# Attention beside a dense layer: odd heads' scores in a step of their own, and a new order of the loads

## The chip, the cores and the metric

One NeuronCore of a Trainium2 chip runs the whole program. Its engines work side by side, each through its own instructions in order: TensorE (PE, matmuls into PSUM; PEld is its weight load), VectorE (DVE), ScalarE (ACT), GpSimd (POOL) and SyncE (SP), which here only issues DMAs and waits for what they need. The metric is the time of one execution on the device in microseconds, the median of several runs.

## The reference, cut to what matters

Three layers follow each other. The first is a gated linear attention (mLSTM): for each of 4 batches and 8 heads a state C of 40 x 40 is carried over 768 positions.

```
for t in range(S):
    m_new = max(f_gate[t] + m, i_gate[t])
    f_stab, i_stab = exp(f_gate[t] + m - m_new), exp(i_gate[t] - m_new)
    C = f_stab * C + i_stab * outer(v[t], k[t]);  n = f_stab * n + i_stab * k[t]
    y[t] = sigmoid(o_gate[t]) * (C @ q[t]) / max(abs(n @ q[t]), 1)
```

Then a dense layer over all 3072 positions of width 320, `relu(x @ w_in)**2 @ w_out` with 2048 hidden columns, and at last a layer of 8 experts in which each position goes to the one with the largest logit: `gate * relu(x @ w1[e]) @ w2[e]`.

## The kernel before, in words

**Chunks.** The attention is done by chunks of 128 positions, 6 for each of the 4 batches, 24 in all, numbered 0 to 23 in the order in which they are worked on. Within a chunk the recurrence becomes matmuls: scores of all pairs of positions (k against q, for each head), times a decay matrix that is the exponential of a masked sum of gates, times the values; to that comes what the state C carries in from the chunk before.

**Names.** st are a chunk's rows of k and q as loaded (two tiles, 120 x 1024 each, in two buffers, so room for one chunk), q3 another copy of q, kvo the rows of k, v and of the gate o (two buffers), Ab the two tiles of decay rows (even and odd heads; four buffers, so room for two chunks). kq holds k and q split into a rounded part and what is left, for exact scores in TensorE's faster format. It has one buffer: line 637 (ScalarE) writes the rounded part of k or q, and four instructions of line 640 (GpSimd) the rest.

**Steps.** `Main.STEPS` cuts a chunk's work into nine steps, of which the last three run beside the first three of the next chunk. Before: step 0 `inter` (the state's part, on TensorE) and all 8 `scores` (line 774: even heads into one PSUM tile sp, odd heads into another), step 1 `weigh0` (VectorE, line 779: even scores times decays) and `scaled`, step 2 `weigh1`, `gate` and `update`, step 3 `update_masked` and `values0`, step 4 `carried` and `values1` (line 787), step 5 `divided`, then `gated` (lines 832 and 833), `turned` (line 835, transposes xpt on TensorE, lines 720 and 722) and `out`. `half` runs one step of the last three of the chunk before (`rest`), then one step of the chunk, and then `prepare`.

**Preparation.** `prepare(n, h)` says what is asked for behind step h of chunk n. `causal` adds and masks decay rows on GpSimd (lines 668 and 669), `decay` takes their exponential on ScalarE (line 675), `decays` loads Ab (line 647), `kvo` (line 616) and `qk` (lines 627 and 630: st and q3) load rows, `round` makes kq. In a chunk of the loop `round(n + 1, 0)` stands behind step 1, `round(n + 1, 1)` behind step 2.

**The dense layer beside it.** It runs in groups of 3 chunks, 16 blocks f to a group. `l1` (line 859) makes 8 matmuls into hp; ScalarE makes g and gh of it (lines 867, 868), VectorE gl (lines 876, 879); `l2` (lines 892 to 894) makes 9 matmuls of gh and gl into the accumulators. Two blocks of `l1` are issued ahead of `l2` (AHEAD = 2). `fin` closes a group: logits lp (line 957), ranks (line 1024), stores of x_d (line 1052).

**Order.** The order on every engine is that in which the code writes the instructions. The chunks 0 to 6 and the first dense blocks follow a list written by hand (PLAN, where the word `sc` calls a chunk's scores); from chunk 7 on `attend` spreads the steps evenly between the dense blocks (STEP = 0.7 of a step at each call, two calls a block). SP's DMAs have that order too, and an issue that has to wait for its buffer holds up the ones behind it.

**PSUM.** Three of eight banks hold the accumulators; all other tiles (hp, sp, tp, pv, xpt, lpt, lp, pr) share the five buffers of psa. A new tile waits until the last reader of the tile that had its buffer is done.

Of the kernel before, what the change touches and what calls it, by code (L numbers as in the profile page):

```python
# [9 lines left out]
F32 = mybir.dt.float32  # L10
# [14 lines left out]
B, H, S, D = 4, 8, 768, 40  # L25
L = 128
# [350 lines left out]
def kernel(ctx, tc, qk, q3, kvo, gates, w_io, wg, w12, cst, out, dbg=None):  # L377
# [8 lines left out]
    def pool(name, bufs, to, **kw):  # L386
        p = tc.tile_pool(name=name, bufs=bufs, **kw)
        to.append(p)
        return p.__enter__()
# [5 lines left out]
    psa = pool("psa", 5, early_ps, space=PSUM)  # L395
# [288 lines left out]

    def prepare(n, h):

        todo = {1: [], 2: [(n + 1, "causal", 0)], 3: [(n + 2, "decays"), (n + 1, "causal", 1), (n + 1, "decay", 0)],
                4: [(n + 1, "decay", 1)], 5: [(n + 1, "weighted")]}
        if n > 0:
            todo[KVO].append((n + 1, "kvo"))  # L690
        if n < WHOLE:
            todo[QK0].append((n + 1, "qk"))
        if n + 1 >= WHOLE:
            for j in range(2):
                todo[(ROUND0 if n < WHOLE else ROUND1)[j]].append((n + 1, "round", j))
            todo[QK1].append((n + 2, "qk"))
        for m, name, *a in todo.get(h, []):
            if m < NC:
                ahead(m, name, *a)
# [3 lines left out]
    def ahead(m, name, *a):  # L703
        if (m, name, *a) not in over:
            over.add((m, name, *a))
            assert name != "decay" or m < AT_ONCE or (m, "causal", *a) in over
            getattr(chunks[m], "decays_early" if name == "decays" and m < AT_ONCE else name)(*a)
# [27 lines left out]
    class Main:  # L735


        STEPS = (("inter", "scores"), ("weigh0", "scaled"), ("weigh1", "gate", "update"), ("update_masked", "values0"),
                 ("carried", "values1"), ("divided",), ("gated",), ("turned",), ("out",))

        def __init__(self, n):
# [10 lines left out]
        def step(self, k):  # L752
            for part in self.STEPS[k]:
                self.run(part)

        def finished(self, k):
            return all(part in self.done or (self.c == 0 and part in ("inter", "scaled", "carried")) for part in self.STEPS[k])

# [4 lines left out]
            if self.last and self.b + 1 < AT_ONCE:  # L763
                nc.sync.dma_start(out=C.rearrange("p g n -> p (g n)"), in_=C_d[self.b + 1])

        def scores(self):
            n, d = self.n, self.d
            assert n < WHOLE or all((n, "round", j) in over for j in range(2))
            for r in range(2):
                self.sps.append(psa.tile([128, 4, L], F32, tag="a", name="sp"))  # L770
            for h in range(H):
                c = slice(L * h, L * h + L)
                k, q = (d.st[j][:, c] for j in range(2)) if n < WHOLE else (d.kq[:, j, c] for j in range(2))
                nc.tensor.matmul(self.sps[h % 2][:, h // 2], k, q, start=True, stop=True)  # L774
# [343 lines left out]
    mains = [Main(n) for n in range(NC)]  # L1118
# [4 lines left out]
    def turn(x, *a):  # L1123
        if count[x] < len(turns[x]):
            fn, i = turns[x][count[x]]
            count[x] += 1
            fn(i, *a)
# [7 lines left out]
    def rest():  # L1135

        n, k = tails
        if n < NC and steps[0] >= PERIOD * (n + 1):
            mains[n].step(PERIOD + k)
            tails[:] = (n, k + 1) if PERIOD + k + 1 < len(Main.STEPS) else (n + 1, 0)  # L1140

    def catch_up():

        while steps[0] < PERIOD * NC and mains[steps[0] // PERIOD].finished(steps[0] % PERIOD):
            steps[0] += 1
        while steps[0] >= PERIOD * (tails[0] + 1) and mains[tails[0]].finished(PERIOD + tails[1]):
            n, k = tails
            tails[:] = (n, k + 1) if PERIOD + k + 1 < len(Main.STEPS) else (n + 1, 0)
        for i in range(steps[0]):
            prepare(*divmod(i, PERIOD))  # L1150
# [18 lines left out]
    def half(n):  # L1169

        if steps[0] < evac(n):
            n, h = divmod(steps[0], PERIOD)
            rest()
            step()
            prepare(n, h)
# [5 lines left out]
    with tc.manual_schedule():  # L1181
# [30 lines left out]
        def layer1():  # L1212
            q = l1(*its[nl[0]])
            gs[nl[0]] = next(q)
            late.append(q)
            late_of[nl[0]] = [q, 0]
            nl[0] += 1

        def layer2():
            i = nd[0]  # L1220
            g, f = its[i]
            if f == 0:
                accs[g] = accumulators()

            if g == NG - 1 and f >= NF - 3:
                l2(g, accs[g], range(2), f, *gs[i])
            elif g == NG and f >= NF0 - 3:
                l2(g, accs[g], [0], f, *gs[i])
                hook()
            else:  # L1230
                for t in range(3):
                    l2(g, accs[g], [t], f, *gs[i])
                    if g == NG:
                        hook()
                gs.pop(i)
            nd[0] += 1
            if (g, f) == (FETCH, 0):
                x = nc.sync.value_load(e0, min_val=0, max_val=E - 1)
                nc.sync.dma_start(out=raw.rearrange("p (o n) -> p o n", o=1), in_=w12[bass.ds(x, 1)].rearrange("o p n -> p o n"))
            if f == NF - 1:  # L1240
                if g == NG - 1:
                    for j in range(i - 2, i + 1):
                        l2(g, accs[g], [2], its[j][1], *gs.pop(j))
                q = fin(g, accs.pop(g))
                next(q)
                before = list(fins)
                fins.append(q)
                if g == NG - 2:
                    leave(brief)
                    p0 = ctx.enter_context(tc.tile_pool(name="p0", bufs=1, side="right"))  # L1250
                    w0.extend([p0.tile([128, WN], F32R, name="w0h"), p0.tile([128, W1], F32R, name="w01l")])
                    fins.append(first_unit(before, p0))
                if g == NG - 1:
                    leave(dense)
                    fins[:] = [last_tokens(q)]
# [27 lines left out]
        def last_tokens(q):  # L1283
# [82 lines left out]
            for j in range(3):  # L1366
# [3 lines left out]
            rest_of.update(idx=idx, xs=xs, gts=gts)  # L1370

        names = dict(kv="kvo", qk="qk", de="decays", ca="causal0", cb="causal1", ea="decay0", eb="decay1", vw="weighted", ra="round0", rb="round1")
        parts = {"in": "inter", "sc": "scores", "wa": "weigh0", "sd": "scaled", "wb": "weigh1", "th": "gate", "up": "update", "um": "update_masked",
                 "va": "values0", "cc": "carried", "vb": "values1", "di": "divided", "ga": "gated", "tu": "turned", "ou": "out"}
        turn_of = {"A": ("A",), "R": ("R",), "T": ("T",), "TP": ("T", "pool"), "TQ": ("T", "psum"), "S": ("S",), "SA": ("S", "scalar"), "W": ("W",), "H": ("H",), "L": ("L",), "LV": ("L", True)}

        def token(word):
            k = len(word.rstrip("0123456789"))
            name, i = word[:k], int(word[k:] or 0)
            if name in turn_of:  # L1380
                x, *a = turn_of[name]
                assert count[x] == i, (word, count[x])
                turn(x, *a)
            elif name in names:
                what = names[name]
                ahead(i, *((what[:-1], int(what[-1])) if what[-1].isdigit() else (what,)))
            elif name in parts:
                mains[i].run(parts[name])
            elif name == "g":
                next(gt)  # L1390
            elif name == "f":
                for _ in range(i):
                    nc.tensor.matmul(apart, ones, ones.rearrange("p (o n) -> p o n", o=1).to_broadcast([128, 4, 128]), start=True, stop=True)
            elif name == "l":
                assert nl[0] == i
                layer1()
            elif name in ("sa", "sb", "sbP"):
                if name == "sbP":
                    on_pool.add(its[i])
                late_of[i][1] += 1  # L1400
                assert late_of[i][1] == (1 if name == "sa" else 2)
                next(late_of[i][0])
                if name != "sa":
                    late.remove(late_of[i][0])
            elif name == "m":
                assert nd[0] == i
                layer2()
            else:
                {"z": constants, "dt": carry}[name]()
# [3 lines left out]
        for word in PLAN:  # L1413
            token(word)
        late.sort(key=lambda q: [i for i in late_of if late_of[i][0] is q])
        catch_up()
        while nd[0] < len(its):
            i = nd[0]
# [135 lines left out]
```

## Time and profile before

| | |
|---|---|
| median of 3 runs | 770.36 us (764.28, 770.36, 772.28) |
| the profiled execution | 762.73 us, of which the span from the first to the last instruction is 760.8 us |
| TensorE | busy 737.1 us (97%), 5197 matmuls |
| VectorE / ScalarE / GpSimd | busy 488.1 / 415.4 / 360.4 us (64 / 55 / 47%) |
| mean granted TensorE clock | 0.993 of full speed |
| DMA | 108.99 MB, 143 GB/s on average |

Busy shares are means over stages with different limits. The opening and the chunks run to some 430 us, the rest of the dense layer to some 530 us, then come the experts. TensorE's matmuls overlap, so its busy time hides small delays; idle time of an engine before an instruction is shown in brackets with what ended it. A wait ended by several events is put down to the last of them.

### The profile page before, as it was taken

Reading aid. Unit: us, or ns where it says so; the run is one execution under the profiler, and the core shown is the slowest. Engines: PE = TensorE matmul, PEld = TensorE weight load, DVE = VectorE, ACT = ScalarE, POOL = GpSimd, SP = SyncE. Lnnn points to the kernel's source line nnn. Section 1 sums busy time; section 2 is a strip of 40 time slices with the busy share of each in tenths; the row PEclk is TensorE's granted clock in tenths of the full one; section 3 lists DMA queues with packets and bytes.
Section 4 is the critical chain, followed back from the end, with each engine's and each line's share of the span. In section 5 each row is a group of like instructions: output and inputs, shape, how many; then the busy total and the mean of one; then the engine's idle time right before and its main releaser. Section 6 shows DMA issues by size and latency. Waiting matters only on the chain.

```text
span 760.8 us, 14426 instructions
## 1 busy us (share of the span) xinstructions
PE 737.1 (97%) x5197; PEld 722.0 (95%) x5198; DVE 488.1 (64%) x1140; ACT 415.4 (55%) x807; POOL 360.4 (47%) x411
## 2 busy tenths in 40 slices
PE   9999999899999999999999999999899999999995
PEld 6799999899999999899989999999799999999995
DVE  8899875865865765565495554454375665777453
ACT  4688865445455545434545435563374556776453
POOL 7658855566446524543554000530246324666540
PEclk9999999999999999999999999999999999999999
DMA  7788844548544444453441000100198556766720
GB/s 245 246 238 262 254 107 120 150 127 271 160 112 129 119 136 111 116 151 104 131 113 69 2 33 1 33 33 33 39 340 265 168 168 204 239 197 197 240 52 14
DMA packets 55043, 108.99 MB, mean 143 GB/s; under 512 B 6896, under 2 KB 34681, under 8 KB 54834
## 3 DMA queue, kind: packets, MB, share of 16 engines
q1 hardware_dynamic: 50370, 95.88, 42.1%
q0 software_dynamic: 4160, 11.77, 4.9%
q8 instruction: 47, 0.77, 0.4%
q10 hardware_dynamic: 432, 0.29, 0.1%
q14 instruction: 34, 0.28, 0.1%
HBM read 98.69 MB, written 10.86 MB: 144 GB/s over the span
## 4 chain that ended last, share of the span: by engine, by line
PE 53%; DVE 4%; DMA 2%; POOL 2%; issue 2%; ACT 1%; SPq 0%; DVEq 0%; POOLq 0%; ACTq 0%
PE hp L291 13%; PE hp L859 12%; PE acc L892 4%; PE acc L894 4%; PE op L310 4%; PE op L312 4%; PE op L311 4%; PE acc L893 4%; DMA st<-in_qk_dram 2%; PE xp L277 1%; PE pv L787 1%; POOL kq L640 1%; PE lp L957 1%; DVE w01l L162 1%; PE sp L774 0%
## 5 line engine op out<-in xcount | busy, mean ns | idle before, releaser
L640 POOL TENSOR_TENSOR kq<-st,kq 120x256 fp32r<-120x256 f32 x136 | 96.2, 740 | 74.7 <-ACT kq L637 71.3
L892 PE MATMUL acc<-w_h,gh 128*128 128x320 f32 x384 | 124.7, 325 | 0.0
L894 PE MATMUL acc<-w_h,gl 128*128 128x320 f32 x384 | 118.9, 310 | 0.0
L893 PE MATMUL acc<-w_l,gh 128*128 128x320 f32 x384 | 118.4, 308 | 0.0
L859 PE MATMUL hp<-xh,w_h 128*128 128x384 f32 x384 | 113.3, 349 | 4.3 <-DVE xh L733 1.6
L867 ACT ACTIVATE g<-hp 128x384 f32<-128x384 f32 x128 | 62.0, 485 | 97.6 <-PE hp L859 93.5
L876 DVE SCALAR_TENSOR_TENSOR hp<-hp,g 128x384 f32<-128x384 f32 x126 | 70.5, 560 | 65.9 <-ACT g L867 65.6
L260 DVE SCALAR_TENSOR_TENSOR gl<-hp,gh 128x384 fp32r<-128x384 f32 x88 | 47.6, 553 | 68.1 <-ACT gh L230 67.7
L859 PE MATMUL hp<-xh,w_l 128*128 128x384 f32 x384 | 87.8, 336 | 0.0
L859 PE MATMUL hp<-xl,w_h 128*128 128x384 f32 x256 | 87.1, 340 | 0.0
L879 DVE TENSOR_TENSOR gl<-hp,gh 128x384 fp32r<-128x384 f32 x126 | 70.3, 558 | 14.1 <-DVE hp L876 0.5
L893 PEld LDWEIGHTS acc<-w_l,gh 128*128 128x128 f32 x384 | 72.5, 189 | 0.0
L892 PEld LDWEIGHTS acc<-w_h,gh 128*128 128x128 f32 x384 | 72.4, 189 | 0.0
L894 PEld LDWEIGHTS acc<-w_h,gl 128*128 128x128 f32 x384 | 72.2, 188 | 0.0
L859 PEld LDWEIGHTS hp<-xh,w_h 128*128 128x128 f32 x384 | 65.7, 190 | 5.4 <-ACT signs L563 1.8
L868 ACT ACTIVATE gh<-g 128x384 fp32r<-128x384 f32 x128 | 67.2, 525 | 4.6 <-PE acc L893 0.5
L859 PEld LDWEIGHTS hp<-xh,w_l 128*128 128x128 f32 x384 | 69.3, 189 | 0.0
L230 ACT ACTIVATE gh<-hp 128x384 fp32r<-128x384 f32 x88 | 43.2, 491 | 39.1 <-PE hp L291 38.2
L637 ACT ACTIVATE kq<-st,cs 120x1024 fp32r<-120x1024 f32 x34 | 39.0, 1146 | 39.5 <-DMA st<-in_qk_dram 35.8
L675 ACT ACTIVATE Ab<-Ab 128x512 f32<-128x512 f32 x42 | 26.2, 628 | 54.0 <-POOL Ab L669 53.9
L681 POOL TENSOR_TENSOR vw<-kvo,wT 128x378 f32<-128x378 f32 x20 | 17.6, 879 | 77.3 <-DMA kvo<-in_kvo_dram 57.0
L173 POOL DMA_INDIRECT out_dram<-ot,idx x34 | 40.1, 1180 | 27.0 <-ACT ot L209 19.6
(291 smaller groups left out, 1861.4 us busy)
## 6 DMA issues: line engine op xcount, KB each, us to landing
st<-in_qk_dram SPq DMA_DIRECT2D x34, 480.0 KB
raw<-in_w_dram SPq DMA_DIRECT2D x30, 512.0 KB, 4.9
kvo<-in_kvo_dram SPq DMA_DIRECT2D x24, 529.0 KB
raw<-in_w_io_dram SPq DMA_DIRECT2D x16, 704.0 KB
Ab<-A_d SPq DMA_DIRECT2D x42, 256.0 KB
raw<-in_w_dram SPq DMA_DIRECT2D x20, 427.0 KB, 4.4
raw<-in_w_dram SPq DMA_DIRECT2D x10, 426.0 KB, 4.3
q<-in_q_dram SPq DMA_DIRECT2D x20, 180.0 KB
```

Source lines behind the costliest of these rows:

```text
L230: e.activation(out=gh[:, j], in_=hp[j % 4], func=ACTF.Relu).then_inc(sGH, 1)
L260: e.scalar_tensor_tensor(out=gl[:, j], in0=hp[j % 4], scalar=0.0, in1=gh[:, j].bitcast(F32), op0=ALU.max, op1=ALU.subtract).then_inc(sGL, 1)
L291: m = e.matmul(hp[f % 4][:, 0:w], a, c, start=(n == 0), stop=(n == 7))
L640: nc.gpsimd.tensor_tensor(out=o[:, c], in0=self.st[j][:, c], in1=o[:, c].bitcast(F32), op=ALU.subtract)
L859: nc.tensor.matmul(hp, a, x, start=(n == 0), stop=(n == 7))
L867: nc.scalar.activation(out=r, in_=hp, func=ACTF.Relu)
L868: nc.scalar.activation(out=gh, in_=r, func=ACTF.Square)
L876: e.scalar_tensor_tensor(out=sq, in0=hp, scalar=0.0, in1=r, op0=ALU.max, op1=ALU.mult)
L879: e.tensor_tensor(out=gl, in0=sq, in1=gh.bitcast(F32), op=ALU.subtract)
L892: nc.tensor.matmul(acc[t][:, 0:DM], gh[:, sl], wh, start=(f == 0), stop=False)
L893: nc.tensor.matmul(acc[t][:, 0:DM], gh[:, sl], wl, start=False, stop=False)
L894: nc.tensor.matmul(acc[t][:, 0:DM], gl[:, sl], wh, start=False, stop=end)
```

## The change

The odd heads' scores move from step 0 to step 1 of a chunk, behind `weigh0` and `scaled`; each PSUM tile sp is taken when its four heads are due. In `prepare`, the decay rows of chunk n + 2 are asked for behind step 4 instead of step 3, so that in SP's queue `kvo` of n + 1 and `qk` of n + 2 (step 3) come first. PLAN keeps its words: `sc` now calls both halves one after the other, even heads first.

```
     def prepare(n, h):
-        todo = {1: [], 2: [(n + 1, "causal", 0)], 3: [(n + 2, "decays"), (n + 1, "causal", 1), (n + 1, "decay", 0)],
-                4: [(n + 1, "decay", 1)], 5: [(n + 1, "weighted")]}
+        todo = {1: [], 2: [(n + 1, "causal", 0)], 3: [(n + 1, "causal", 1), (n + 1, "decay", 0)],
+                4: [(n + 2, "decays"), (n + 1, "decay", 1)], 5: [(n + 1, "weighted")]}
...
-        STEPS = (("inter", "scores"), ("weigh0", "scaled"), ("weigh1", "gate", "update"), ("update_masked", "values0"),
+        STEPS = (("inter", "scores0"), ("weigh0", "scaled", "scores1"), ("weigh1", "gate", "update"), ("update_masked", "values0"),
...
-        def scores(self):
+        def scores(self, r):
             n, d = self.n, self.d
             assert n < WHOLE or all((n, "round", j) in over for j in range(2))
-            for r in range(2):
-                self.sps.append(psa.tile([128, 4, L], F32, tag="a", name="sp"))
-            for h in range(H):
+            self.sps.append(psa.tile([128, 4, L], F32, tag="a", name="sp"))
+            for h in range(r, H, 2):
...
+            elif name == "sc":
+                mains[i].run("scores0")
+                mains[i].run("scores1")
```

## Rows read from the trace of the kernel before

**Rows 1.** Busy us (and instructions) by engine, clock, DMA share, GB/s, 105 to 430 us

```profile
105.00:430.00 325.00, 316.69 (x2218) 313.14 (x2217) 209.62 (x549) 162.00 (x322) 157.69 (x229) 0.99 0.44 127
```

**Rows 2.** Waits of TensorE, 105 to 430 us: us in total, times, longest

```profile
PE sp L774 <- DVE gl L879: 2.5, 2, 1.3
PE sp L774 <- DVE kvo L833: 1.8, 1, 1.8
...
PE hp L859 <- DVE kvo L833: 0.8, 2, 0.5
```

**Rows 3.** Timeline of TensorE, chunk 9: start, us, instruction, count, idle before and releaser

```profile
141.78 0.30 PE L774 MATMUL sp<-kq 120*128 120x128 f32 x1
143.90 0.97 PE L774 MATMUL sp<-kq 120*128 120x128 f32 x7 [1.81 <-DVE kvo L833]
144.97 0.61 PE L859 MATMUL hp<-xh,w_h 128*128 128x384 f32 x2
```

**Rows 4.** Timeline of TensorE, chunk 18

```profile
310.12 0.22 PE L774 MATMUL sp<-kq 120*128 120x128 f32 x1
311.47 1.00 PE L774 MATMUL sp<-kq 120*128 120x128 f32 x7 [1.13 <-DVE gl L879]
312.30 0.78 PE L957 MATMUL lp<-wgs,scr 128*128 128x8 f32 x6
```

**Rows 5.** Timeline of TensorE, chunk 22

```profile
395.15 0.31 PE L774 MATMUL sp<-kq 120*128 120x128 f32 x1
396.79 1.00 PE L774 MATMUL sp<-kq 120*128 120x128 f32 x7 [1.34 <-DVE gl L879]
397.62 0.36 PE L892 MATMUL acc<-w_h,gh 128*128 128x320 f32 x1
```

**Rows 6.** As rows 1, around and behind three score stalls; the clock is third from last

```profile
141.80:146.00 4.20, 2.28 (x17) 2.03 (x16) 3.83 (x18) 0.00 (x0) 0.82 (x1) 1.00 0.97 230
313.80:317.20 3.40, 3.40 (x13) 3.40 (x13) 0.36 (x1) 1.15 (x1) 1.11 (x2) 0.50 0.34 89
395.10:401.00 5.90, 4.56 (x33) 4.39 (x32) 4.56 (x11) 1.91 (x4) 1.10 (x2) 1.00 0.97 272
```

**Rows 7.** Waits of ScalarE, 105 to 430 us

```profile
ACT Ab L675 <- POOL Ab L669: 53.9, 23, 3.9
...
ACT kq L637 <- DMA st<-in_qk_dram: 35.8, 12, 4.8
```

**Rows 8.** Timeline of TensorE, chunk 8

```profile
125.49 1.09 PE L774 MATMUL sp<-kq 120*128 120x128 f32 x8
126.41 0.56 PE L859 MATMUL hp<-xh,w_h 128*128 128x384 f32 x2
...
127.97 0.38 PE L722 MATMUL xpt<-cs,kvo 128*128 128x128 f32 x2
```

**Rows 9.** Timeline of ScalarE, chunk 8: the first rounding for chunk 9

```profile
128.61 1.15 ACT L637 ACTIVATE kq<-st,cs 120x1024 fp32r<-120x1024 f32 x1 [4.45 <-DMA st<-in_qk_dram]
```

**Rows 10.** Timeline of TensorE, chunk 22: the transposes of step 1

```profile
399.10 0.38 PE L722 MATMUL xpt<-cs,kvo 128*128 128x128 f32 x2
```

**Rows 11.** Timeline of ScalarE, chunk 22: the first rounding for chunk 23

```profile
399.49 1.15 ACT L637 ACTIVATE kq<-st,cs 120x1024 fp32r<-120x1024 f32 x1 [3.69 <-PE xpt L722]
```

**Rows 12.** Timeline of SP's DMA issues, chunks 7 and 8

```profile
120.69 0.88 SPq L627 DMA_DIRECT2D st<-in_qk_dram  x2
...
134.74 2.68 SPq L647 DMA_DIRECT2D Ab<-A_d  x2
137.47 0.49 SPq L616 DMA_DIRECT2D kvo<-in_kvo_dram  x1
138.13 0.86 SPq L627 DMA_DIRECT2D st<-in_qk_dram  x2
```

**Rows 13.** Timeline of GpSimd, chunks 8 and 9: last subtractions for 9, mask for 10

```profile
134.40 2.82 POOL L640 TENSOR_TENSOR kq<-st,kq 120x256 fp32r<-120x256 f32 x4
...
151.64 1.04 POOL L668 TENSOR_TENSOR Ab<-Ab,cT 128x512 f32<-128x512 f32 x1
```

More of the change, by code (lines that the diff above doesn't have):

```diff
@@ L1372 @@
         names = dict(kv="kvo", qk="qk", de="decays", ca="causal0", cb="causal1", ea="decay0", eb="decay1", vw="weighted", ra="round0", rb="round1")
-        parts = {"in": "inter", "sc": "scores", "wa": "weigh0", "sd": "scaled", "wb": "weigh1", "th": "gate", "up": "update", "um": "update_masked",
+        parts = {"in": "inter", "wa": "weigh0", "sd": "scaled", "wb": "weigh1", "th": "gate", "up": "update", "um": "update_masked",
                  "va": "values0", "cc": "carried", "vb": "values1", "di": "divided", "ga": "gated", "tu": "turned", "ou": "out"}
```

## The prediction

> **What bounds the kernel now.** I went first to where TensorE is not busy. The planned opening ends at about 105 us; the 17 chunks that a loop places (numbers 7 to 23) run beside the dense layer from there to about 430 us, and in that stretch TensorE is busy 316.69 of 325.00 us, 97% [rows 1]. VectorE stands at 65% there, ScalarE and GpSimd at half. So the changed steps can give back 8.3 us of idle time, and what a lowered clock costs. The order after 430 us is untouched.
>
> The waits of TensorE in that stretch say what the 8.3 us are [rows 2]: 2.5 and 1.8 us before the score matmuls of line 774 and 0.8 us before hp of line 859, ended by VectorE's lines 879 and 833. Those instructions don't make what the scores read; they are the last readers of older PSUM tiles. TensorE waits for a free one of psa's five buffers. The timeline shows the form: in chunk 9 the first even score starts at 141.78 and the first odd one at 143.90 [rows 3], in chunk 18 at 310.12 and 311.47 [rows 4], in chunk 22 at 395.15 and 396.79 [rows 5]. It is the second score tile that comes too late. Scores follow each other at 0.11 us (eight take 0.92 [rows 8]), so the three stalls are 2.0, 1.2 and 1.5 us.
>
> Then the other engines: ScalarE waits 35.8 us for st, the rows of the next chunk, and 53.9 us for GpSimd's causal masks [rows 7]. It works in order, so g and gh of the dense layer wait behind; but TensorE runs two dense blocks ahead (AHEAD), and none of its waits in rows 2 names g or gh. Last SP's queue: the second decay load waits for values1, and kvo and st are issued behind it [rows 12].
>
> **The change, part by part.**
>
> Split scores, chunk 22: after the four even scores TensorE would go on to nine l2 matmuls, some 1.4 us (397.62 to the transposes at 399.10 [rows 5, 10]), which need no PSUM buffer. The missing one came free just ahead of 396.79, before those end at 395.15 + 0.45 + 1.4 = 397.0. All 1.5 us go.
>
> Chunk 9: behind the even scores comes hp, and it asks for the buffer for which the odd scores waited. It starts at 143.90 instead of 144.97 [rows 3], and four scores (0.45 us) are owed a step later: 1.07 - 0.45 = 0.6 us.
>
> Chunk 18: lp takes that buffer, at 311.47 instead of 312.30 [rows 4]: 0.83 - 0.45 = 0.4 us.
>
> The two waits of hp for line 833 (0.8 us [rows 2]) go, since one score tile less is held then. So far 1.5 + 0.6 + 0.4 + 0.8 = 3.3 us. Does the odd tile wait for a buffer in its new place? weigh0 and scaled, ahead of it in program order, free two, and a whole step lies between: 0. At worst the 4.3 us of rows 2 before scores come again there.
>
> The clock: behind the stall of chunk 18 it was granted at half, 1.2 GHz, from 313.8 to 317.2, which costs 3.4 x 0.5 = 1.7 us; behind the longer stall of chunk 9 and that of chunk 22 it stayed at 2.4 GHz [rows 6]. Since two thirds of the stall in chunk 18 stay by the sum above, I take 0; the ends are 0 and -1.7. [...]
>
> The price of the split: kq has one buffer, so the rounding of the next chunk (line 637 on ScalarE, then four subtractions on GpSimd) may start only after the odd scores. Those would stand right behind the transposes xpt of step 1. In chunk 8 these end at 128.35 [rows 8]; with 0.55 us for the odd scores that makes 128.9, against 128.61 for line 637 before [rows 9]. In chunk 22 it is 399.48 + 0.55 = 400.0 against 399.49 [rows 10, 11]. Over the 15 chunks from 8 to 22, taken in this way from the timeline, the new start is later in nine, by 10.2 us together, and earlier in six, by 3.1: 7.1 us on balance, 0.5 each. So **the earlier st buys nothing**: until now ScalarE waited for st, now it waits for the odd scores at about the same time. How much of ScalarE's delay reaches TensorE? 35.8 + 53.9 = 89.7 us of it [rows 7] stand beside at most 8.3 us on TensorE, 9%. So 7.1 x 0.09 = +0.6 us; the ends are 0 and +10.2, all of the late ones passed on.
>
> One more change of group on TensorE per chunk: seven scores and what follows take 0.83 us [rows 4], eight 0.92 [rows 8], so a change costs at most 0.83 - 7 x 0.09 = 0.2; at 0.11 a score it is some 0.03. 16 x 0.03 = +0.5 us; the ends are 0 and +3.2.
>
> kvo, st and q3 ahead of the decays: the first half of st is freed by the first four subtractions, the second only by the last four, which in chunk 8 end at 137.2 [rows 13]. Until now st was issued at 138.13, behind the decay loads (134.74 to 137.42) and kvo [rows 12]. So the second half gains 1 us, the first and kvo some 3 to 5. No wait of TensorE is ended by any of them: 0.
>
> The decays, one step later: in SP's queue they now stand behind the wait for the second half of st and the issues of st and q3, and go out at about 139 instead of 134.7 and 137. Their first user, the mask of line 668, runs at 151.64 [rows 13], so 12 us cover it: 0. If the cover is gone, GpSimd waits, and behind it ScalarE at the exponentials. The stores of x_d on the same queue swap places with them by one step, and nothing moves on GpSimd's or ScalarE's queue: 0.
>
> In the planned opening the eight scores stay together, even ones first: 0.
>
> Sum: -3.3 + 0 + 0.6 + 0.5 = **-2.2 us**, against the profiled execution's 762.73 us: 760.5. That execution lies 7.6 us below the median shown (770.36); with this difference carried over the forecast is 768 us.
>
> **The rivals.**
>
> Full recovery: all waits of TensorE go, because SP's new order also takes the worst lateness out of ScalarE and GpSimd, and the clock stays up: -8.3 - 1.7 = -10.0, 760.4 us. For it: most waits in rows 2 end with VectorE, which runs late behind ScalarE. Against it: the start of the rounding hardly moves.
>
> It does nothing: hp and lp take over the waits in full, as they do by two thirds in chunks 9 and 18, and st stays bound by GpSimd: 770.4 us.
>
> Slower, through kq: ScalarE, in order, holds g and gh behind line 637 until the odd scores are done. It decides where the way from the even scores to the transposes is longer than st took; that is so in nine chunks. If each such delay reaches TensorE and nothing of the 3.3 is kept, +10.2: 780.6 us. For it: 53.9 us of waits for masks [rows 7] say that GpSimd's chain behind the rounding is tight. Against it: waits of up to 4.8 us for st [rows 7] ended in no stall named by g or gh.
>
> Late decays: the loads queue behind kvo, st and q3. From its issue at 120.69 [rows 12] to the end of ScalarE's wait at 128.61 [rows 9] st took 7.9 us; by the same time the decays land at 139 + 7.9 = 147, 5 us ahead of line 668. If they took twice that, 154.8, GpSimd would be 3.2 us late in 14 chunks, 45 us, of which 9% is +4.0, and with +1.1 for the split's prices and -3.3 kept: 772.2 us. [...]
>
> **How the numbers follow.** Forecast 0.48, full recovery 0.22, nothing 0.12, kq 0.13, late decays 0.05. About 1% (7.7 us) is what a measurement of this kernel tells from no change; its three times lie between 764.28 and 772.28. Faster than 762.7: most of full recovery (0.17) and low draws of the forecast (0.05), 0.22. Slower than 778.1: 0.11 of kq and 0.02 of the others, 0.13. Within: 0.65. The range, 758 to 778, reaches to full recovery less 2 and three quarters of the way to kq, and leaves out some 0.1 on either side.
>
> **What would show it.** Right: no gap between the first and the second score in chunks 9, 18 and 22, but waits of 0.8 to 1.5 us before hp in chunk 9 and lp in chunk 18; line 637 released by line 774, and ScalarE's waits for st gone; line 668 never waiting for a decay load. Wrong: idle time of TensorE from 105 to 430 us under 3 us (full recovery), or over 12 us (kq); decay loads that end GpSimd's waits.

## The result, and the profile after

Six executions of the changed kernel have a median of 759.12 us (757.36 to 762.82), six of the kernel before on the same chip 768.06 us. The ratio is 0.9872 (95% interval 0.9842 to 0.9902): 1.3% faster, some 9 us where 2 were forecast. On another chip the same kernel, run again as e4 below, gave 756.06 against 763.1 us, 0.9921 (0.9889 to 0.9952). Both intervals hold a gain of 1.0 to 1.1%, and neither holds the forecast's 0.3%. The ratios, here and below, are not the quotients of the medians, from which they differ by up to 0.2%.

The profiled execution after is the slowest of its six, 762.82 us with a span of 761.0 against 760.8 before, so spans don't show the gain; the stretch that the change touches does. The first view is VectorE's group of line 778, which weighs the scores (line 779 before; behind the edit the kernel after counts one line less): count, ns (least, median, most), first start to last end. Of before:

```profile
L779 DVE TENSOR_TENSOR Ab<-sp,Ab x34: 678/692/693, 108.7 to 427.2; 128x512 f32<-128x512 f32 x34
```

Of after:

```profile
L778 DVE TENSOR_TENSOR Ab<-sp,Ab x34: 681/692/693, 110.6 to 422.3; 128x512 f32<-128x512 f32 x34
```

The same 34 weighs take 311.7 instead of 318.5 us: 6.8 us less. 1.7 of it is the fall of the clock at 313.8 us [rows 6], which this execution doesn't have there; **5.1 us** are left. What hides them in the span: the weighs start 1.9 us late, behind a stretch of half clock at 39 us in the opening, and the start of the experts takes 5.2 us longer, 1.7 of them by a stretch of half clock that lies in it (last section). Below, "saved" means this stretch from the first weigh to the last, with 1.7 us for each stretch of half clock inside it set aside, against 318.5 - 1.7 = 316.8 us before. It comes from one profile of each kernel; the two profiles of the changed kernel, after and e4, differ by 0.2 us in it.

The windows of after that answer to rows 1 and rows 6, in their columns: the whole stretch, then around the scores of chunks 18, 9 and 22 where they now lie:

```profile
105.00:430.00 325.00, 321.17 (x2266) 318.34 (x2265) 214.86 (x562) 164.75 (x325) 158.85 (x232) 1.00 0.47 128
...
306.00:320.00 14.00, 13.76 (x103) 13.47 (x101) 8.03 (x28) 6.89 (x14) 6.56 (x10) 1.00 0.51 127
143.00:147.00 4.00, 2.78 (x21) 2.66 (x20) 3.60 (x15) 0.52 (x1) 0.00 (x0) 1.00 0.51 133
390.00:396.00 6.00, 4.86 (x36) 4.60 (x35) 5.22 (x15) 2.24 (x4) 0.28 (x1) 1.00 0.74 211
```

TensorE's idle time went from 8.3 [rows 1] to 3.8 us, and the clock stays at 2.4 GHz throughout. The longest waits of TensorE there, after (us in total, times, longest):

```profile
PE hp L858 <- DVE kvo L832: 1.2, 1, 1.2
PE xpt L720 <- DVE kvo L832: 1.1, 1, 1.1
PE hp L858 <- ACT scr L951: 0.7, 3, 0.2
```

No score waits any more; the 4.3 us of rows 2 before line 774 are gone. One wait stands before hp and one before the transposes xpt, as the timeline of TensorE shows for chunks 9, 18 and 22 (beside [rows 3 to 5]):

```profile
143.95 0.64 PE L773 MATMUL sp<-kq 120*128 120x128 f32 x4
145.82 0.59 PE L858 MATMUL hp<-xh,w_h 128*128 128x384 f32 x2 [1.22 <-DVE kvo L832]
...
310.11 0.56 PE L773 MATMUL sp<-kq 120*128 120x128 f32 x4
310.51 0.78 PE L956 MATMUL lp<-wgs,scr 128*128 128x8 f32 x6
...
390.38 0.64 PE L773 MATMUL sp<-kq 120*128 120x128 f32 x4
390.86 0.36 PE L891 MATMUL acc<-w_h,gh 128*128 128x320 f32 x1
...
393.53 0.30 PE L720 MATMUL xpt<-cs,kvo 128*64 128x128 f32 x1 [1.14 <-DVE kvo L832]
```

And the waits of ScalarE after, which answer to rows 7:

```profile
ACT Ab L675 <- POOL Ab L669: 55.8, 25, 3.9
ACT g L866 <- PE hp L858: 48.3, 39, 4.0
ACT kq L637 <- PE sp L773: 39.6, 16, 4.2
```

ScalarE stands as long as before at line 637 (35.8 us for st and 3.7 for xpt before, together 39.5); only the releaser is another. In chunk 8 the first rounding starts at 130.53, behind the odd scores, where it started at 128.61 behind st [rows 9]; GpSimd's mask for chunk 10 runs at 153.53 instead of 151.64 [rows 13], and no decay row is waited for. Both are 1.9 us later, as much as this execution is late from the opening on (the first weigh at 110.6 instead of 108.7), so against the rest of the chunk neither moved. The two rows of after:

```profile
130.53 1.15 ACT L637 ACTIVATE kq<-st,cs 120x1024 fp32r<-120x1024 f32 x1 [4.19 <-PE sp L773]
```

```profile
153.53 1.05 POOL L668 TENSOR_TENSOR Ab<-Ab,cT 128x512 f32<-128x512 f32 x1
```

### The profile page after: what moved, and what is told of

Same layout as the page of the kernel before. It is cut to its first block, busy times and chain, and to the rows that moved or that the text cites. A ratio compares the mean times of both kernels' runs of the same rounds, so it can differ in the third digit from the quotient of the medians.

```text
span 761.0 us, 14439 instructions
## 1 busy us (share of the span) xinstructions
PE 739.4 (97%) x5197; PEld 724.0 (95%) x5198; DVE 490.1 (64%) x1140; ACT 416.7 (55%) x807; POOL 360.7 (47%) x411
## 5 line engine op out<-in xcount | busy, mean ns | idle before, releaser
L875 DVE SCALAR_TENSOR_TENSOR hp<-hp,g 128x384 f32<-128x384 f32 x126 | 70.6, 560 | 64.2 <-ACT g L866 64.0
L878 DVE TENSOR_TENSOR gl<-hp,gh 128x384 fp32r<-128x384 f32 x126 | 70.3, 558 | 13.7
L891 PEld LDWEIGHTS acc<-w_h,gh 128*128 128x128 f32 x384 | 72.3, 188 | 0.0
L637 ACT ACTIVATE kq<-st,cs 120x1024 fp32r<-120x1024 f32 x34 | 39.1, 1149 | 39.6 <-PE sp L773 39.6
L675 ACT ACTIVATE Ab<-Ab 128x512 f32<-128x512 f32 x42 | 26.1, 626 | 56.0 <-POOL Ab L669 55.8
L786 PEld LDWEIGHTS pv<-kvo,Ab 128*128 128x128 f32 x384 | 48.4, 191 | 0.5
```

The source lines that it names most:

```text
L786: nc.tensor.matmul(self.pv[:, hd], d.Ab[r][:, i], d.v[:, hd], start=True, stop=True)
L875: e.scalar_tensor_tensor(out=sq, in0=hp, scalar=0.0, in1=r, op0=ALU.max, op1=ALU.mult)
L878: e.tensor_tensor(out=gl, in0=sq, in1=gh.bitcast(F32), op=ALU.subtract)
L891: nc.tensor.matmul(acc[t][:, 0:DM], gh[:, sl], wh, start=(f == 0), stop=False)
```

## The experiments

Two explanations stood at the outset. By P, the theory of the prediction, TensorE is held by PSUM buffers, and asking for one score tile less at a time is what helps; the load order does nothing. By its rival (Q in what was expected), the new order of SP's loads takes lateness out of ScalarE (through st, S) or out of what needs values (through kvo, K). Each kernel ran in five rounds beside the kernel before; e1 to e4 share one chip, e5 to e8 a second, e9 to e11 a third.

### e1: the split alone, with the old order of loads

```
-        todo = {... 3: [(n + 1, "causal", 1), (n + 1, "decay", 0)], 4: [(n + 2, "decays"), (n + 1, "decay", 1)], ...}
+        todo = {... 3: [(n + 2, "decays"), (n + 1, "causal", 1), (n + 1, "decay", 0)], 4: [(n + 1, "decay", 1)], ...}
```

> Only the scores are split over steps 0 and 1; the decay rows are asked for in step 3 as before. Theory P (a free PSUM buffer at the scores is what was missing): all of the gain, ratio 0.985 to 0.992; TensorE idles under 5 us of the stretch from 105 to 430 us (8.3 before), no gap inside the scores, line 637 ends its waits with the odd scores. Theory Q (the order of SP's queue brings the gain): ratio 0.998 to 1.010, since st still comes as late as before and kq is free later; ScalarE's waits for st stay at some 30 us and more. Theory both-needed: between, 0.993 to 0.998.

Measured: 758.5 against 763.1 us, 0.995 (0.9922 to 0.9977); 2.9 us saved. ScalarE's waits at line 637, of e1:

```profile
ACT kq L637 <- DMA st<-in_qk_dram: 29.2, 8, 5.0
ACT kq L637 <- PE sp L773: 20.1, 8, 4.2
```

The split gives about what the forecast put on it, and not all of the gain, as P had it: the ratio lies where both parts were said to be needed. It also makes ScalarE stand 49.3 us at line 637, 9.8 more than before: half the time st is last, half the odd scores.

### e2: the new order of loads alone, scores together

```
-        todo = {... 3: [(n + 2, "decays"), (n + 1, "causal", 1), (n + 1, "decay", 0)], 4: [(n + 1, "decay", 1)], ...}
+        todo = {... 3: [(n + 1, "causal", 1), (n + 1, "decay", 0)], 4: [(n + 2, "decays"), (n + 1, "decay", 1)], ...}
```

> Only the loads are put in the new order (decay rows in step 4); all eight scores stay in step 0. Theory P: ratio 0.997 to 1.003, the gaps before the second score stay at 1 to 2 us in some three chunks, TensorE idles 7 to 10 us from 105 to 430 us, although ScalarE's waits for st fall from 35.8 us to under 5. Theory Q: ratio 0.985 to 0.993 and the gaps go, because ScalarE and with it VectorE run earlier. Late decays: ratio over 1.003 with GpSimd's line 668 waiting for the decay loads.

Measured: 753.1 against 763.1 us, 0.9883 (0.9851 to 0.9915); **6.9 us saved**, more than with the split beside it (5.1, and 5.3 in e4). The windows of e2, and its waits of ScalarE:

```profile
105.00:430.00 325.00, 322.29 (x2278) 319.80 (x2277) 213.19 (x560) 165.84 (x326) 157.01 (x229) 1.00 0.46 128
```

```profile
ACT g L867 <- PE hp L859: 84.9, 57, 4.3
ACT Ab L675 <- POOL Ab L669: 41.1, 19, 3.2
ACT kq L637 <- PE sp L774: 11.4, 7, 2.4
```

How far ScalarE holds up VectorE shows in VectorE's waits for it, for g and for the rounded columns xh, before a PSUM tile (hp or xpt) is emptied. Before:

```profile
DVE hp L876 <- ACT g L867: 40.8, 33, 3.5
DVE xl L732 <- ACT xh L731: 31.5, 12, 4.8
```

and in e2:

```profile
DVE hp L876 <- ACT g L867: 36.3, 33, 3.1
DVE xl L732 <- ACT xh L731: 27.9, 12, 3.7
```

Together they fall from 72.3 to 64.2 us. St is never waited for, and 39.5 us at line 637 became 11.4. Instead ScalarE waits for hp (52.4 us before): it is now on time for the dense layer. TensorE's idle time fell from 8.3 to 2.7 us, and the stalls before the scores to one of 0.7 us, though the scores still stand together. The ratio is the one expected under Q, and it contradicts the prediction's "the earlier st buys nothing". Why st is early shows in SP's queue. Its waits before:

```profile
SPq L647 <- PE pv L787: 142.6, 26, 15.7
SPq L647 <- DVE Ab L779: 53.6, 13, 8.8
```

and after (the first two):

```profile
SPq L627 <- POOL kq L640: 86.5, 27, 4.1
SPq L627 <- ACT kq L637: 41.5, 20, 9.4
```

Before, SP stood 196 us in the decay loads' issue (line 647) until values1 (142.6 us) or the weighing (53.6) was done with their buffer, with st's issue queued behind; now st goes as soon as its own buffer is free.

### e3: even heads first, then odd ones, both in step 0

The old order of loads, and:

```
-        STEPS = (("inter", "scores0"), ("weigh0", "scaled", "scores1"), ...
+        STEPS = (("inter", "scores0", "scores1"), ("weigh0", "scaled"), ...
```

> Both halves of the scores in step 0, even heads first, the odd tile taken after the fourth score; loads in the old order. It has the new order of the eight scores, without the odd ones coming a step later. Theory P: ratio 0.997 to 1.003, the gap now lies behind the fourth score instead of the first, of the same 1 to 2 us less 0.35. If the order of the eight scores itself (even ones done four matmuls sooner, weigh0 starting sooner) brought the gain: 0.985 to 0.993.

Measured: 762.21 against 763.1 us, 0.9986 (0.9957 to 1.0015); 0.1 us saved. Going through one tile before the other is worth nothing; it's the step between the halves that counts.

### e4: the changed kernel once more

No edit: the kernel after, beside e1 to e3 on their chip.

> The changed kernel unaltered, for its profile and the granted clock of each run. Theory P with the clock (the score stalls let the granted clock fall in many runs, which costs more than the idle time): the times of both kernels order themselves by their mean clock, before at 0.980 to 0.993, changed at 0.990 to 0.997, and at equal clock the changed kernel is 2 to 5 us shorter. If the clock has no part: both have the same mean clock and the ratio of 0.987 stands at equal clock. The wait of some 5 us at 548 to 557 us that the first profile of the changed kernel shows behind the branch into the experts is an accident of that run and is not seen again.

Measured: 756.06 us, 0.9921 (0.9889 to 0.9952), 5.3 us saved. Against e1 (0.995) the order adds 2.2 to 2.4 us behind the split; against e2 (0.9883) the split *costs* 1.6 to 1.8. The whole time agrees: the slowest execution of e2 (754.63 us) is faster than the fastest of e4 (754.79).

### e5, e6, e7: which of the three loads matters

All with the scores together and the decays in step 3 again; only the sequence of the three issues in that step differs (before: decays, kvo, qk).

```
+        loads = ['qk', 'decays', 'kvo']       # e5;  e6: kvo, decays, qk;  e7: kvo, qk, decays
+        todo[3] = [x for x in todo[3] if x[1] not in loads] + sorted((x for x in todo[3] if x[1] in loads), key=lambda x: loads.index(x[1]))
```

> Scores together in step 0; in step 3 SP is asked for st and q3 first, then the decay rows, then kvo, so that of the two loads that the new order brings forward only st comes early. Theory S (the order's gain is ScalarE's wait for st: without it VectorE runs earlier and frees PSUM buffers in time): most of the gain of the order alone (0.9883), 0.987 to 0.991; ScalarE's waits for st under 8 us in the stretch from 105 to 430 us, TensorE idle 2 to 4 us there. Theory K (the gain is GpSimd's wait for kvo, 51 us before, which delays its masks): 0.996 to 1.002.

> Scores together in step 0; in step 3 SP is asked for kvo first, then the decay rows, then st and q3: of the two loads only kvo comes early. Theory S: 0.996 to 1.002, ScalarE's waits for st stay at 30 us or more. Theory K: 0.987 to 0.991, GpSimd's waits for kvo under 10 us and its masks earlier (ScalarE waits for them under 45 us).

> Scores together in step 0; SP's order as in the changed kernel (kvo, st, q3, decay rows), but the decay rows are asked for behind step 3, not step 4. If only the order within SP's queue counts: the same as the order alone, 0.986 to 0.991. If the later step itself counts: over 0.993 or under 0.985.

Measured, against 769.45 us: e5 760.58 us, 0.9868 (0.9835 to 0.9901), 5.9 saved; e6 759.41, 0.9879 (0.9847 to 0.9911), 6.0 saved; e7 758.83, 0.9852 (0.9825 to 0.988), 6.9 saved. In e5 kvo goes out last, and GpSimd, which weighs the values, waits for it (51.4 us before):

```profile
POOL vw L681 <- DMA kvo<-in_kvo_dram: 61.0, 9, 9.3
```

These 61 us cost at most the 1.0 us by which e5 saves less than e7, so K is not what brings the gain. E7 is e2 without the later step: the decays' step is worth nothing, their place behind st is all. E6 went against S as I had put it, and its ratio is the one expected under K: with st still last I expected its waits to stay, but they fell:

```profile
ACT kq L637 <- DMA st<-in_qk_dram: 14.4, 9, 2.8
```

So e6 doesn't tell K from S; e5 does. The gain of e6 goes with ScalarE's standing time (39.5 to 20.4 us with all releasers). Why st comes earlier there with the decay loads still ahead of it I didn't settle.

### e8: the order alone, and the rounding one step later

```
-QK0, QK1, ROUND0, ROUND1 = 1, 3, (3, 4), (1, 2)
+QK0, QK1, ROUND0, ROUND1 = 1, 3, (3, 4), (2, 3)
```

> The order alone (scores together), but both roundings of the next chunk one step later (behind steps 2 and 3), so line 637 comes as late as the split makes it, or later, while ScalarE is free before it. Theory kq (the split costs what it does because the rounding starts later and GpSimd's masks with it): most of the gain is lost, 0.993 to 1.000, ScalarE waits for masks over 55 us (41.1 in the order alone). Rival (the split costs because ScalarE stands blocked in front of line 637): 0.986 to 0.990, as the order alone.

Measured: 759.58 against 769.45 us, 0.9871 (0.9839 to 0.9903), 5.7 saved. I expected the gain to be lost again if an early rounding were its cause. It was not: what helps is not that kq is ready early. ScalarE waits nowhere at line 637 here, and for the masks only 18.3 us. That left the reading that its *standing* is the harm. The next three test that.

### e9: the kernel before, with the rounding one step later

The edit of e8 alone: scores together, loads in the old order.

> The kernel before with its old order of loads and unsplit scores, only both roundings of the next chunk one step later (behind steps 2 and 3), so that st has landed when ScalarE comes to line 637. Theory S (ScalarE's standing wait for st delays VectorE, which frees PSUM buffers late): 5 to 6 us of the order's gain without touching the loads; the attention (first to last weigh in the loop, 318.5 us before) shortens by 4 to 6 us, ScalarE's waits for st fall under 10 us. Rival (the order gains through the transfers themselves): no gain, ratio 0.998 to 1.003, as GpSimd's chain only starts later.

Measured: 758.3 against 769.25 us, 0.986 (0.9827 to 0.9894); **6.8 us saved** without anything of the change. The waits of ScalarE in e9:

```profile
ACT g L867 <- PE hp L859: 126.8, 63, 4.5
ACT Ab L675 <- POOL Ab L669: 17.3, 12, 2.2
```

St is as late as before, but ScalarE takes up the rounding only when its rows are there, and does g and gh meanwhile. The stalls before the scores shrink from 4.3 to 1.0 us without a load moved. But e9 moves more than line 637: GpSimd's part of the rounding goes along, so the mask of line 668 for chunk 10 now runs ahead of the subtractions of line 640, at 145.66, where it ran behind them at 151.64 [rows 13], and ScalarE's waits for masks fall from 53.9 to 17.3 us. So e9 shows that ScalarE's waiting is the harm, not at which of the two lines. GpSimd and the windows in e9:

```profile
145.66 1.04 POOL L668 TENSOR_TENSOR Ab<-Ab,cT 128x512 f32<-128x512 f32 x1
...
149.21 2.88 POOL L640 TENSOR_TENSOR kq<-st,kq 120x256 fp32r<-120x256 f32 x4 [1.79 <-ACT kq L637]
```


```profile
105.00:430.00 325.00, 322.27 (x2277) 319.73 (x2276) 212.66 (x561) 164.33 (x326) 157.13 (x230) 1.00 0.45 127
```

### e10: the order alone, and ScalarE held for as long as it used to stand

The first rounding of a chunk placed by the loop is done three times over, with the same values.

```
-            nc.scalar.activation(out=o, in_=self.st[j], func=ACTF.Copy, scale=third[:, j:j + 1])
+            for _ in range(3 if j == 0 and self.n > WHOLE else 1):
+                nc.scalar.activation(out=o, in_=self.st[j], func=ACTF.Copy, scale=third[:, j:j + 1])
```

> The order alone, but ScalarE does the first rounding of every chunk of the loop three times over (the same result), so it and GpSimd behind it are held for 2.3 us more at line 637, about what the wait for the odd scores is in the changed kernel (38.9 us in 16 waits). Theory S: 2 to 4 of the 6.9 us that the order saves in the attention are lost again. If ScalarE's delay costs TensorE nothing: under 0.7 us lost.

Measured: 776.01 against 769.25 us, 1.0075 (1.0047 to 1.0103). The group of the weighs, the windows at the three falls of the clock and the waits of TensorE in e10:

```profile
L780 DVE TENSOR_TENSOR Ab<-sp,Ab x34: 678/691/692, 109.5 to 434.8; 128x512 f32<-128x512 f32 x34
```

```profile
165.00:168.50 3.50, 3.50 (x15) 3.40 (x14) 1.79 (x4) 3.21 (x3) 0.15 (x1) 0.52 0.18 48
318.60:322.00 3.40, 3.40 (x13) 3.40 (x12) 0.36 (x1) 2.19 (x2) 1.10 (x2) 0.50 0.01 2
403.90:407.30 3.40, 3.40 (x15) 3.30 (x14) 1.97 (x4) 3.33 (x3) 0.00 (x0) 0.50 0.15 38
```

```profile
PE sp L775 <- DVE gl L880: 4.9, 3, 2.3
PE hp L860 <- DVE kvo L834: 2.4, 2, 1.4
PE sp L775 <- DVE kvo L834: 1.8, 1, 1.8
```

Some 37 us more of ScalarE (16 chunks x 2 x 1.15 us) bring back the pattern of rows 2, with the same releasers, and more of it. VectorE waits longer for ScalarE, 82.6 us against 64.2 in e2:

```profile
DVE hp L877 <- ACT g L868: 47.1, 34, 4.1
DVE xl L733 <- ACT xh L732: 35.5, 12, 4.7
```

GpSimd's part is held up with it, and ScalarE's waits for masks rise from 41.1 to 57.5 us. With 5.1 us for three falls set aside the stretch takes 320.2 us, 10.3 more than in e2, 28% of the 37. I had expected 2 to 4 to be lost.

### e11: the changed kernel, and the rounding one step later

The edit of e8 on the kernel after.

> The changed kernel with both roundings one step later, so ScalarE no longer stands in front of line 637 for the odd scores. If that standing wait is what the split costs on top of the order (5.5 us saved in the attention with both, 6.9 with the order alone): 6 to 7.5 us saved, 1 to 2 us better than the changed kernel. If the later start of the rounding is the cost: at most 5.5 saved.

Measured: 758.02 against 769.25 us, 0.9852 (0.982 to 0.9884); **8.3 us saved**, the most of all, and more than the 6 to 7.5 expected. The windows and the waits of TensorE in e11:

```profile
105.00:430.00 325.00, 323.69 (x2290) 321.27 (x2289) 214.72 (x562) 165.31 (x328) 157.15 (x229) 1.00 0.46 128
```

```profile
PE sp L773 <- DVE gl L878: 0.6, 1, 0.6
...
PE hp L858 <- DVE kvo L832: 0.2, 1, 0.2
```

1.3 us of idle time are left of 8.3, less than in any other run here. It beats the kernel before, and by the stretch the kernel after; its ratio and that of after in the result (0.9872) have overlapping intervals, so the whole time doesn't yet separate those two.

All eleven in one table, with three sums of waits from 105 to 430 us: "line 637", ScalarE there, all releasers; "masks", ScalarE for GpSimd's masks; "VectorE", VectorE for ScalarE's g and xh:

| kernel | scores split | loads | rounding | line 637, us | masks, us | VectorE, us | saved, us |
|---|---|---|---|---|---|---|---|
| before | no | old | early | 39.5 | 53.9 | 72.3 | 0 |
| e3 | no | old | early | 42.0 | 54.8 | 76.3 | 0.1 |
| e1 | yes | old | early | 49.3 | 56.2 | 77.1 | 2.9 |
| after, e4 | yes | new | early | 39.6, 38.9 | 55.8, 55.0 | 72.7, 73.2 | 5.1, 5.3 |
| e5, e6, e7 | no | three other sequences | early | 11.5, 20.4, 11.4 | 47.7, 46.3, 41.1 | 66.0, 66.0, 64.4 | 5.9, 6.0, 6.9 |
| e2 | no | new | early | 11.4 | 41.1 | 64.2 | 6.9 |
| e8 | no | new | late | 0 | 18.3 | 64.8 | 5.7 |
| e9 | no | old | late | 0 | 17.3 | 64.7 | 6.8 |
| e11 | yes | new | late | 0 | 16.2 | 63.1 | 8.3 |
| e10 | no | new | early, ScalarE held | 13.4 + 37 busy | 57.5 | 82.6 | -3.4 |

Among the kernels without the split what is saved goes with VectorE's waits: 64 to 66 us where 5.7 to 6.9 are saved, 72 to 76 where nothing is, 82.6 in e10. Line 637 and the masks alone don't order them: e8 and e9 have hardly any of either and save no more than e2. Why e8 saves some 1 us less than e2 and e9 is open.

## Why the prediction was right or wrong

**The range holds the time, and that is luck in part.** 759.12 us lies in 758 to 778, but 9 us below the forecast, where the range reached to a rival. Most signs named for the forecast came true as well: no gap between the scores, hp waiting in chunk 9, line 637 released by the odd scores, no decay load waited for. They couldn't tell the sum from its rival; e1 and e2 do.

**The bound: right.** TensorE was held by PSUM tiles whose last readers on VectorE came late; every kernel that gained lost some of these waits, and e10 made them return. One reader was left out: 1.6 of the 8.3 us before were ended by ScalarE's line 952, which copies a PSUM tile out, 1.4 of them here:

```profile
PE hp L859 <- ACT scr L952: 1.4, 1, 1.4
```

In e1, where ScalarE stands longer, that line ends 2.7 us of TensorE's waits; in e2 and e9, none.

**The split's terms: right in sum, not in each place.** Forecast for the split with its prices -2.2 us; alone (e1) it saves 2.9. That agreement is luck in part: in e1 ScalarE stands 9.8 us longer than before, and in after, where it stands as long as before, the same split leaves 5.1. So the split's own gain was taken too small, and in e1 the longer standing, which the sum didn't have, took the difference away. In chunk 9 hp waits 1.22 us, inside the 0.8 to 1.5 named. In chunk 18 lp was to wait 0.8 us and doesn't. In chunk 22 the gap between the scores is gone, but 1.14 us come back a little later, before the transposes of step 1, which I had not counted.

**"The earlier st buys nothing", 0 us: this is the step that failed.** Its first half was right: against before, ScalarE stands about as long at line 637 (39.5 and 39.6 us), released by the odd scores. Its second half was wrong. The split alone would have made it 49.3 us; the order takes 9.7 of them off and so 2.2 us, and without the split 28.1 off and 6.9. The parts don't add (2.9 + 6.9 against 5.1), since the split hands part of the order's gain back: with st early, what ScalarE waits for is the odd scores. Where nothing makes it stand at line 637, the split is worth 1.5 to 2.6 us more (e11 against e9 and e8).

**The pass-on of 9%: mis-sized.** I divided TensorE's stalls by all of ScalarE's waits, the 53.9 us for masks among them, and read "none of its waits in rows 2 names g or gh" as cover. But a late g shows under another name: VectorE comes to gl late, behind it to line 833, and TensorE is released by these. The cleanest price is that from e1 to after, where the waits for masks stay at 56 us: 2.2 us for 9.7 of standing at line 637, 23%, and still 12% if the 1.0 us that kvo can have cost in e5 is taken off. So 9% was too low for line 637, by how much is open. The 7.1 us that it was applied to came out as 0.1 (39.5 to 39.6 us of standing). Put down to line 637 alone, e9 gives 17% (6.8 of 39.5), e2 25% (6.9 of 28.1) and e10 28%, but there the waits for masks moved as well; with them e9 comes to 9% (6.8 of 76.1), e2 to 17% (6.9 of 40.9) and e10 to 19% (10.3 of 55.4). What the runs show directly is that ScalarE's held time is the cause and that VectorE's waits for it move along; they don't part line 637 from the masks in e9, and the loads are only one way to change it.

**The clock, 0 us: wrong.** The profiles of e1, e2 and after show no fall from 105 to 430 us, but neither does e3's, whose stalls stayed, so one profile of each settles nothing. Over the runs of e4 and of the kernel before beside it, the time lost to a lowered clock (span times what the mean clock lacks of full) has a mean of 4.8 us before and 3.3 in e4: -1.5 us. There the sum is then 5.3 + 1.5 = 6.8 of the 7.0 us by which the medians differ. The other runs agree: e2 loses 2.0 us beside the 4.8, e5 to e9 and e11 lose 4.5 to 5.4 beside 7.2 to 7.7, e10, whose stalls came back, 10.7 beside 7.2; and in each of e1 to e11 "saved" and this difference add up to within 1.9 us of the difference of the medians. The Trainium skill (TensorE: Matmul & The Clock Gate, section "A second HAM failure mode: psum-queue depth-cycling") tells of another kernel whose short idles between groups of matmuls, from cycling through PSUM, made the clock go up and down and cost throughput. The time lost here moves in that direction, and the end of -1.7 us was nearer than my 0.

**The decays: right.** They go out at 140.06 us (forecast: about 139; this execution is 1.9 us late), here in SP's timeline of after, beside rows 12:

```profile
134.61 4.89 SPq L627 DMA_DIRECT2D st<-in_qk_dram  x2
139.55 0.40 SPq L630 DMA_DIRECT2D q<-in_q_dram  x1
140.06 0.94 SPq L647 DMA_DIRECT2D Ab<-A_d  x2
```

and GpSimd never waits for them. In e8 it does, 47.1 us, and in e11 53.4; even so 5.7 and 8.3 us are saved.

**The rivals.** Full recovery (760.4 us) lay nearest to 759.12, and its reason holds: the order takes lateness out of ScalarE. The recovery isn't full, though: 3.8 of the 8.3 us of idle time are left, and the medians differ by 8.9 and 7.0 us and not by 10.0. E2, without the split, comes to 10.0. The objection I held against it, that the start of the rounding hardly moves, was true of before against after and beside the point. Slower through kq has the right mechanism, and its price is real, 1.7 us between e2 and after, but measured against a gain and not against before.

## What to carry to other kernels

When an engine that works in order feeds the release of PSUM tiles, cost its standing time by an experiment that moves its instruction (as e9 does, but see which of its other waits move along) or holds it longer (e10), not by what the waiting engine names. Look at the engine between the two as well: here VectorE's waits for ScalarE went with what each kernel saved. A wait that stands in front of other work is a matter of where the instruction is put as much as of when its data come. In a queue of DMA issues, put the one that must wait longest for its buffer last. Try the parts of a change alone: here one half gave more without the other.

## What the hardware showed that I had not expected

At the start of the experts some executions take 4 to 6 us longer. The profile of after has it at 547 to 558 us:

```profile
DVE gl L260 <- issue: 3.9, 1, 3.9
```

"Issue" means that the engine waited for nothing that the profile shows. From the end of the last matmul ahead of the experts (line 1470 before) to the first of line 310 it is 10.0 us in the profiles of before and e1 to e4, 14.7 to 15.6 in those of after and e5 to e10, 13.7 in e11. Part of that is the clock: in all of the longer ones but e11 TensorE falls to 1.2 GHz behind its waits there (in after from about 554.3 to 557.7 us, where a matmul of line 291 takes 0.41 us instead of 0.28); e11 has no fall there, so some 3.7 us are the wait itself. The same kernel has it on one chip (after) and not on another (e4). I had called it an accident that would not come again; it goes with the chip or the run and not with the edit, and its cause is open. The kernel before is slower on the chips of after and e5 to e11 as well (768.06, 769.45 and 769.25 against 763.1 us); no profile shows it there, so that it has the wait too is likely and not shown. That is why only ratios on one chip are compared here.
